# Causal block attention followed by a gated unit: an earlier padding, another first load, joined score groups and a new order

## The chip, the cores and the metric

The kernel runs on one core of a Trainium2 chip. The metric is the device time of one execution in microseconds (us); several executions are timed and their median is given. A profile comes from one further execution, which has a time of its own. The engines are PE (TensorE; its weight loads are a row of their own, PEld), DVE (VectorE), ACT (ScalarE), POOL (GpSimd) and SP (SyncE, which here only issues transfers).

## What is computed

Eight batches, eight heads, 576 tokens, head size 64. Attention is causal by blocks of 64 tokens. Its output, with the heads side by side as 512 features, goes through a unit in which a causal convolution of five taps and a sigmoid gate a linear map, and a second linear map follows. Cut from the reference:

```python
scores = scale * np.matmul(q, k.transpose(0, 1, 3, 2))
mask = block_i >= block_j                      # blocks of 64 tokens
attn = exp(scores - max) / sum                 # where mask
x = (attn @ v) as [8, 576, 512]
gate = sigmoid(sum over kk of conv_w[kk] * x shifted by 4 - kk)
out = (gate * (x @ w_val)) @ w_out
```

## The kernel before

**Units of work.** Four heads form a quad (16 quads, numbered `a`), two heads a pair (32 pairs, `p`). Two batches form a unit of the second half, cut into thirteen token tiles (`n`, 288 tokens wide for n 0 to 3, 384 after that) for convolution, gate and value map, and into 37 output tiles.

**Staging of q and k.** `load_qk` (line 179) brings the 128 x 1152 fp32 block of a quad: partition = (head, group of 18 tokens). `cast_qk` (line 214) turns it into fp16 and, while it does, swaps token and feature so that two neighbouring tokens lie side by side; `trans` (line 242) then transposes these pairs as if they were fp32 elements, 576 of them, in blocks of 32 x 32 on DVE. The result, `qT` and `kT`, has 32 features of a head on each of four strips of 32 partitions. `ends` (line 253) copies the first and the last key block into `kz`, beside zeros. The first quad is loaded, cast and transposed in halves (`load_half`, `cast_half`, `trans_half`, words `Lqh`, `cqh`, `tqh`): each half has 10 or 8 of the 18 tokens of every partition, so all four halves are needed before any score can be made.

**Scores.** `scores` (line 257) computes for quad `a` and key tile `t` (0, 1, 2) the transposed scores of four heads, one on each strip of 32 rows of the PE array, into four PSUM banks. Called with a half index it does the heads of two strips alone. t = 0 takes 448 + 64 + 64 columns a pass, t = 1 takes 448 + 64, t = 2 takes 320 + 192; each twice, as a head has 64 features. `exps` (line 273) turns a bank into 512 fp16 columns of `pt` on ACT. `mask` (line 278) is three POOL instructions a pair: a copy of a 64 x 64 corner into the columns 1536 to 1600, and two clears. `av` (line 289) multiplies with v, a column of ones giving the sums; `norm` divides on DVE; `xtrans` and `evac_x` transpose back into `xts`.

**Second half.** `conv` (line 333) makes the five taps with 32 x 32 diagonal weights, as one unit of 80 matmuls into four banks or as halves of 40 into two; `gate` is a tanh on ACT, `val` the value map, `gated` the product on DVE, `proj`, `evac_out` and `store` the output.

**Order.** Nothing is reordered: the text `PLAN` is a list of words such as `s.4.1.0@56` (scores of quad 4, t = 1, half 0, into banks 5 and 6) and is issued word by word. Each engine takes its own instructions in that order, and SP its transfers. Before the plan come nine matmuls on zeros (`warm`), the identity and its fold (line 434, 437, on DVE) and clears; `pads` (line 418, word `pm`) sets the columns of `pt` behind 1536 to one and the first columns of `xts` to zero, by fourteen POOL instructions inside the plan. All loads are issued by SP.

Of the kernel before, what the change touches and what calls it, by code (L numbers as in the profile page):

```python
# [10 lines left out]
Lqh.0.0 Lqh.1.1  # L11
# [3 lines left out]
Lqh.0.1 cqh.0.0@D tqh.0.0 Lqh.1.0 cqh.1.0@A Lcn cqh.1.1@D cqh.0.1@P w@0 w@0 w@0 w@0 cw@0 tqh.1.1  # L15
Lvt.0 tqh.0.1 tqh.1.0 pm kz.0@P s.0.1.0@12 s.0.2@5634 Lqk.1.1 cvt.0 e.0.1.0 e.0.1.1 e.0.2.3 cT
cq.1.1@P Lqk.1.0 s.0.0.1@70 s.0.1.1@12 Lv.1 e.0.2.2 e.0.1.3 tq.1.1 e.0.0.3 e.0.0.2 kz.1@D cq.1.0@P
s.0.0.0@34 DG cv.1 tq.1.0 e.0.1.2 Lqk.2.1 e.0.0.1 m.1 e.0.0.0 s.1.1.1@07 e.0.2.1 Lqk.2.0 s.1.0.1@12
e.0.2.0 e.1.0.3 e.1.0.2 Lv.0 av.1.0@3 cq.2.1@P av.1.1@4 e.1.1.3 n.1.0 s.1.1.0@56 Lv.3 n.1.1 m.0
e.1.1.2 s.1.2.1@31 cv.0 xtr.1@2 av.0.1@4 e.1.2.3 cq.2.0@P tq.2.1 e.1.2.2 cv.3 av.0.0@0 s.1.0.0@71  # L20
e.1.1.0 Lqk.3.0 Lqk.3.1 Lv.2 m.3 kz.2@D e.1.1.1 e.1.0.1 xt.1 tq.2.0 cq.3.0@P n.0.1 n.0.0 s.1.2.0@23
s.2.2.1@56 Lv.5 e.1.0.0 e.1.2.1 Lvt.1 av.3.0@4 av.3.1@1 Lv.4 s.2.1.1@70 e.1.2.0 s.2.0.1@23 n.3.0
e.2.2.3 cq.3.1@P n.3.1 e.2.2.2 xtr.0@4 tq.3.0 e.2.1.3 cv.2 xtr.3@1 xt.0 tq.3.1 e.2.1.2 s.2.0.0@56
m.2 xt.3 e.2.0.3 s.2.1.0@40 av.2.0@7 cv.5 e.2.0.2 kz.3@D Lqk.4.1 e.2.0.0 n.2.0 e.2.0.1 cvt.1
av.2.1@1 s.2.2.0@23 e.2.1.0 m.5 s.3.2.0@56 n.2.1 cv.4 av.5.0@7 e.2.1.1 e.2.2.0 e.2.2.1 xtr.2@1
av.5.1@0 n.5.0 s.3.1.0@42 Lwv.0 e.3.2.1 cq.4.1@P Lqk.4.0 e.3.2.0 s.3.0.0@37 e.3.1.0 s.3.1.1@56
e.3.1.1 e.3.1.2 n.5.1 xt.2 xtr.5@0 m.4 e.3.1.3 tq.4.1 kz.4@D e.3.0.1 cq.4.0@P e.3.0.0 Lwv.1 xt.5
av.4.1@1 Lv.7 av.4.0@2 n.4.0 n.4.1 s.3.0.1@40 e.3.0.3 s.3.2.1@56 Lqk.5.0 m.6 cn.0.0@23 tq.4.0
e.3.0.2 e.3.2.2 e.3.2.3 wv.1@D cn.1.0@71 th.1.1 th.1.0 wv.0@D s.4.0.0@04 cv.7 s.4.1.0@56 s.4.0.1@17
m.7 th.0.1 th.0.0 e.4.1.0 cq.5.0@P val.0.1@2 av.7.0@3 e.4.1.1 Lqk.5.1 val.1.1@5 e.4.0.2 Lvt.2  # L30
e.4.0.0 val.0.0@6 gv.0.1 n.7.0 cn.0.1@23 e.4.0.1 cq.5.1@P gv.1.1 gv.0.0 tq.5.1 s.4.2@4650 e.4.0.3
th.0.3 th.0.2 s.4.1.1@17 e.4.2.1 Lv.6 e.4.2.0 wv.2@D tq.5.0 val.1.0@2 e.4.1.2 Lqk.7.0 Lvt.3 av.7.1@3
cv.6 Lqk.6.0 av.6.0@4 e.4.1.3 wv.3@P m.8 e.4.2.2 gv.1.0 av.6.1@6 n.7.1 e.4.2.3 Lv.11 s.5.2.1@21
e.5.2.3 Lqk.6.1 n.6.0 cn.1.1@73 kz.5@P e.5.2.2 n.6.1 s.5.1@4056 th.1.2 cvt.3 th.1.3 Lv.8 Lwo.2
e.5.1.1 e.5.1.2 xtr.7@1 xtr.4@2 xtr.6@3 e.5.1.0 cv.11 val.0.2@7 Lv.9 xt.7 val.1.3@1 xt.4 s.5.2.0@20
xt.6 e.5.1.3 Lv.10 e.5.2.1 e.5.2.0 gv.1.3 s.5.0@3456 e.5.0.1 e.5.0.0 cvt.2 gv.0.2 val.1.2@1 gv.1.2
val.0.3@7 cn.3.0@02 cq.6.0@P gv.0.3 tq.6.0 e.5.0.2 cq.6.1@P cv.8 Lwo.1 cn.2@4713 tq.6.1 Lwo.0
e.5.0.3 th.2.3 th.2.2 th.3.1 th.3.0 val.2.2@5 th.2.0 cq.7.0@P th.2.1 av.8.1@6 gv.2.2 m.11 val.2.3@1
m.9 n.8.1 tq.7.0 s.6.1@0235 val.3.0@6 av.11.0@4 cv.9 gv.2.3 Lwo.3 Lqk.7.1 av.9.1@7 cv.10 gv.3.0
e.6.1.3 av.8.0@1 n.11.0 Lqk.8.0 av.11.1@6 kz.6@D e.6.1.1 e.6.1.2 e.6.1.0 wo.1@P wo.0@A s.6.2@4035  # L40
n.9.1 cq.7.1@P e.6.2.3 n.8.0 n.11.1 e.6.2.2 cn.3.1@27 m.10 av.9.0@1 xtr.8@6 e.6.2.0 Lqk.8.1 th.3.2
cq.8.0@P val.3.1@3 e.6.2.1 Lqk.9.1 o.0.0@5 th.3.3 n.9.0 s.6.0@4210 oc.0.0@A xt.8 Lvt.4 gv.3.1 Lv.12
val.2.0@6 Lv.14 tq.7.1 xtr.9@7 val.3.3@3 cq.8.1@P Lv.15 e.6.0.3 gv.2.0 e.6.0.2 xt.9 s.7.1@0156
e.6.0.1 e.6.0.0 av.10.1@7 av.10.0@2 e.7.1.2 tq.8.0 xtr.11@4 m.12 Lv.13 kz.7@P st.0.0 cv.12 gv.3.3
Lqk.9.0 o.0.1@3 e.7.1.3 n.10.1 n.10.0 m.13 e.7.1.1 s.7.0@7256 e.7.1.0 Lqk.10.0 oc.0.1@D xt.11 cv.13
cq.9.1@P cq.9.0@P cv.14 tq.8.1 val.3.2@0 xtr.10@1 Lqk.11.0 av.12.0@3 st.0.1 gv.3.2 Lvt.5 val.2.1@4
e.7.0.2 e.7.0.3 xt.10 s.8.2.1@56 e.7.0.0 e.7.0.1 Lv.17 n.12.0 s.7.2@0127 e.8.2.3 av.12.1@3 gv.2.1
av.13.1@4 n.12.1 kz.8@D Lv.19 e.8.2.2 n.13.1 e.7.2.0 av.13.0@5 o.0.2@6 e.7.2.3 e.7.2.1 n.13.0
cn.4@1430 e.7.2.2 cv.15 oc.0.2@D xtr.12@2 th.4.2 xt.12 th.4.0 cvt.4 xtr.13@7 tq.9.1 th.4.3 th.4.1
m.14 xt.13 o.0.5@5 s.8.2.0@62 oc.0.5@D s.8.0@0314 m.15 Lqk.10.1 Lv.18 o.0.4@7 oc.0.4@D e.8.2.1  # L50
tq.9.0 av.14.1@5 e.8.2.0 o.0.6@2 e.8.0.0 st.0.4 kz.9@P cq.10.0@P e.8.0.1 n.14.1 e.8.0.2 s.8.1@3760
Lv.16 e.8.0.3 cv.17 s.9.1.1@14 oc.0.6@D val.4.2@5 av.14.0@2 e.8.1.3 st.0.2 e.8.1.2 val.4.1@0 gv.4.2
n.14.0 e.9.1.3 cq.11.0@P e.9.1.2 s.9.2@1465 e.8.1.0 e.8.1.1 tq.10.0 m.17 e.9.2.2 st.0.6 av.15.1@2
e.9.2.0 xtr.14@3 e.9.2.3 gv.4.1 av.15.0@7 e.9.2.1 n.15.1 val.4.0@0 cq.10.1@P n.15.0 s.9.1.0@25 m.16
Lqk.11.1 e.9.1.0 cv.19 e.9.1.1 Lqk.12.0 s.9.0@6714 xt.14 gv.4.0 cv.18 Lv.22 av.17.1@3 e.9.0.1
tq.10.1 n.17.1 e.9.0.2 cv.16 e.9.0.3 av.16.0@0 n.16.0 m.19 xtr.15@2 o.0.7@5 o.0.3@3 tq.11.0 e.9.0.0
oc.0.3@A s.10.1@4601 xt.15 Lqk.12.1 e.10.1.3 e.10.1.2 s.10.2.1@72 oc.0.7@D kz.10@P e.10.2.3 e.10.1.1
e.10.1.0 Lv.21 val.4.3@5 e.10.2.2 gv.4.3 cvt.5 cq.11.1@P av.19.0@3 av.16.1@0 o.1.2@1 cq.12.0@P
n.19.0 s.10.0@4653 Lv.20 Lvt.7 n.16.1 oc.1.2@A cv.20 e.10.0.3 e.10.0.2 st.0.7 st.0.5 cn.5@7102
cq.12.1@P th.5.3 m.18 Lv.25 th.5.2 av.17.0@3 tq.11.1 th.5.0 val.5.0@5 th.5.1 e.10.0.0 n.17.0  # L60
val.5.3@0 e.10.0.1 gv.5.3 cn.6@2317 Lqk.14.0 s.10.2.0@04 xtr.17@6 st.0.3 gv.5.0 th.6.3 av.18.1@5
th.6.2 tq.12.0 xtr.16@1 th.6.1 av.19.1@7 th.6.0 e.10.2.1 Lv.23 n.18.1 e.10.2.0 kz.11@D Lqk.13.0
# [38 lines left out]
def kernel(  # L101
# [10 lines left out]
    nc = tc.nc  # L112
# [57 lines left out]
    bank = {}  # L170
# [14 lines left out]
    def half(h):  # L185
        return (slice(0, 5), slice(5, 9))[h]
# [289 lines left out]
```

## Time and profile before

| what | value |
|---|---|
| median of three runs | 189.88 us (189.83, 189.88, 193.27) |
| the profiled execution | 188.78 us, of which 186.9 us from first to last instruction (the span) |
| mean granted TensorE clock in the span | 0.958 |
| busy: PE, DVE, ACT, POOL | 168.9, 131.7, 130.0, 104.3 us |
| first matmul of the scores, first exp | 8.03 us, 8.68 us |
| last matmul ends, last store issued | about 182.7 us, about 183.8 us |

Busy time is the union of an engine's instructions. Matmuls overlap, so what a group of matmuls costs is best read from the start of its first to the start of the next group's first. Times inside the span count from its first instruction.

### The profile page before, as it was taken

The numbers are of one execution on the slowest core, as the hardware profiler recorded it, in microseconds if no ns is written. First come the engines' busy times: TensorE is split into PE (matmuls) and PEld (weight loads), VectorE is DVE, ScalarE is ACT, GpSimd is POOL, SyncE is SP. The second block draws the span as 40 slices with busy tenths as digits, with TensorE's granted clock in tenths as the row PEclk, the third lists the DMA queues.
The fourth block names the chain that finished last, engine by engine and source line by source line (L and its number), as shares of the span: only waits on it lengthen the run. The fifth ranks groups of instructions, "written<-read, shape, count | busy, mean of one in ns | idle before, by whom it ended". The sixth has DMA issues, their size and how long they took to land.

```text
span 186.9 us, 8148 instructions
## 1 busy us (share of the span) xinstructions
PE 168.9 (90%) x3433; PEld 111.0 (59%) x3433; DVE 131.7 (70%) x289; ACT 130.0 (70%) x266; POOL 104.3 (56%) x205
## 2 busy tenths in 40 slices
PE   7635999999996899899999689999999999999991
PEld 2323767776775368456667458666666668654440
DVE  6743997968695579788975588966779677832730
ACT  3393899999998187689898467698779865042342
POOL 4898899599966638788466256929074312000000
PEclk9965799999999699999999999999999999999997
DMA  6999899966999789868987999707861023003685
GB/s 202 287 347 284 226 281 383 365 203 166 238 244 402 186 226 349 208 207 221 346 215 157 262 289 297 206 4 237 257 199 61 22 95 117 4 4 112 239 308 187
DMA packets 49407, 40.39 MB, mean 216 GB/s; under 512 B 39253, under 2 KB 39509, under 8 KB 49370
## 3 DMA queue, kind: packets, MB, share of 16 engines
q1 hardware_dynamic: 49226, 39.73, 70.7%
q8 instruction: 27, 0.44, 1.1%
q10 hardware_dynamic: 144, 0.13, 0.2%
q14 instruction: 10, 0.08, 0.1%
HBM read 30.42 MB, written 9.44 MB: 213 GB/s over the span
## 4 chain that ended last, share of the span: by engine, by line
PE 65%; DVE 16%; DMA 5%; issue 5%; POOL 3%; ACT 2%; SPq 0%; ACTq 0%; DVEq 0%; POOLq 0%
PE B L124 62%; DVE kT L243 4%; PE B L310 4%; DVE qT L243 4%; DMA out_dram<-osb 3%; DVE x L303 3%; DMA qks<-in_q_dram 2%; DVE rc L302 1%; DVE xt L316 1%; DVE gv L359 1%; ACT pt L274 1%; POOL qk L228 1%; POOL pt L420 1%; ACT th L348 1%; DVE osb L228 1%
## 5 line engine op out<-in xcount | busy, mean ns | idle before, releaser
L274 ACT ACTIVATE pt<-B 128x512 f16<-128x512 f32 x192 | 98.3, 620 | 19.1 <-PE B L124 16.6
L228 POOL CAST qk<-qks 128x1152 f16<-128x1152 f32 (+1 forms) x31 | 42.3, 1377 | 5.1 <-DMA qks<-in_q_dram 3.9
L124 PE MATMUL B<-qT,kT 32*128 32x448 f16 (+3 forms) x640 | 39.5, 296 | 5.5 <-DVE qT L243 4.0
L124 PE MATMUL B<-v,pt 128*128 128x65 f16 x896 | 35.9, 195 | 2.9 <-issue 2.5
L124 PE MATMUL B<-xt,w_val 128*128 128x384 f16 (+1 forms) x208 | 37.9, 316 | 0.2 <-issue 0.2
L124 PEld LDWEIGHTS <-pt 128*128 128x128 f16 x960 | 33.8, 99 | 7.0 <-issue 4.7
L124 PE MATMUL B<-w_out,gv 128*128 128x512 f16 (+1 forms) x148 | 35.8, 380 | 2.1 <-DVE osb L228 1.1
L359 DVE SCALAR_TENSOR_TENSOR gv<-th,B 128x384 f16<-128x384 f32 (+1 forms) x52 | 26.1, 518 | 11.8 <-PE B L124 11.3
L303 DVE TENSOR_TENSOR x<-B,rc 128x320 f16<-128x320 f32 x64 | 31.5, 492 | 2.5 <-DVE rc L302 0.2
L124 PEld LDWEIGHTS <-kT 32*128 32x128 f16 x640 | 18.1, 94 | 22.2 <-issue 9.2
L348 ACT ACTIVATE th<-B 128x384 f32<-128x384 f32 (+1 forms) x52 | 20.7, 482 | 13.0 <-PE B L124 7.7
L124 PEld LDWEIGHTS <-w_val 128*128 128x128 f16 x208 | 18.3, 98 | 9.7 <-issue 1.2
L280 POOL COPY pt<-pt 64x128 f16<-64x128 f16 x32 | 10.5, 328 | 22.9 <-ACT pt L274 20.0
L124 PEld LDWEIGHTS <-gv 128*128 128x128 f16 x148 | 13.7, 99 | 15.4 <-issue 3.1
L222 POOL CAST v<-vst 128x512 f16<-128x512 f32 x32 | 19.3, 613 | 5.9 <-DMA vst<-in_v_dram 2.8
L243 DVE STREAM_TRANSPOSE kT<-qk 128x576 f32<-128x576 f32 (+2 forms) x17 | 19.7, 1156 | 4.1 <-POOL qk L228 4.1
L228 ACT COPY osb<-B 128x512 f32<-128x512 f32 (+1 forms) x18 | 10.2, 571 | 16.3 <-PE B L124 15.8
L302 DVE RECIPROCAL rc<-B 128x5 f32<-128x5 f32 x64 | 12.0, 188 | 13.5 <-PE B L124 12.0
L228 DVE COPY osb<-B 128x512 f32<-128x512 f32 x19 | 13.1, 688 | 11.2 <-PE B L124 9.0
L243 DVE STREAM_TRANSPOSE qT<-qk 128x576 f32<-128x576 f32 (+2 forms) x17 | 19.7, 1156 | 0.7 <-PE B L124 0.6
L281 POOL MEMSET pt<- 64x384 f16 x32 | 13.2, 413 | 10.3 <-ACT pt L274 8.8
L316 DVE COPY xt<-B 128x576 f16<-128x576 f16 x32 | 14.1, 450 | 4.5 <-PE B L310 4.5
(42 smaller groups left out, 123.3 us busy)
## 6 DMA issues: line engine op xcount, KB each, us to landing
out_dram<-osb SPq DMA_DIRECT2D x35, 256.0 KB, 2.9
qks<-in_k_dram SPq DMA_DIRECT2D x15, 576.0 KB, 6.7
qks<-in_q_dram SPq DMA_DIRECT2D x15, 576.0 KB, 6.9
vst<-in_v_dram SPq DMA_DIRECT2D x64, 128.0 KB, 5.2
vtst<-in_v_dram SPq DMA_DIRECT2D x8, 128.0 KB, 6.4
w_st<-in_moe_w_val_dram SPq DMA_DIRECT2D x2, 512.0 KB, 6.3
w_st<-in_moe_w_out_dram SPq DMA_DIRECT2D x4, 256.0 KB, 5.1
qks<-in_q_dram SPq DMA_DIRECT2D x1, 320.0 KB, 3.0
```

The source lines that it names most:

```text
L124: nc.tensor.matmul(out=out, lhsT=lhsT, rhs=rhs, start=start, stop=stop, skip_group_check=True)
L222: nc.gpsimd.tensor_copy(out=v16s[p % NV][0:128, 0:4, 0:2, 0:64], in_=vst[p % NVS][0:128])
L228: (eng.copy if eng is nc.scalar else eng.tensor_copy)(out=o, in_=i)
L243: nc.vector.transpose(out=(qT, kT)[i][a % NQT][0:128].bitcast(fp32).rearrange("p c (x n) -> p c n x", n=9)[:, :, n], in_=qk16[(2 * a + i) ...
L274: nc.scalar.activation(out=pts[(2 * a + r // 2) % NPT][0:128, r % 2, 512 * t:512 * t + 512], in_=f32(bank["s", a, t, r]), func=AF.Exp, bia ...
L280: nc.gpsimd.tensor_copy(out=pt[64:128, 0:2, 1536:1600], in_=pt[64:128, 0:2, 0:64])
L281: nc.gpsimd.memset(pt[64:128, 0:2, 0:1536].rearrange("p h (t s) -> p h t s", t=3)[:, :, :, 0:64], 0.0)
L302: nc.vector.reciprocal(out=rc[0:128], in_=O[:, :, 64:65])
L303: nc.vector.tensor_tensor(out=x16[p % NX16][0:128, 0:5, h, 0:64], in0=O[:, :, 0:64], in1=rc[0:128].to_broadcast([128, 5, 64]), op=ALU.mult)
L316: nc.vector.tensor_copy(out=xts[b // 2 % NX][0:128, g, b % 2, 4:4 + SEQ], in_=f16(bank["xtr", p])[:, 0:SEQ])
L348: nc.scalar.activation(out=ths[n % NTH][0:128, r, 0:w], in_=f32(bank["cn", n, r])[:, 0:w], func=AF.Tanh, bias=0.0, scale=0.5)
L359: nc.vector.scalar_tensor_tensor(out=gvs[u % 2][0:128, x, t:t + w], in0=ths[n % NTH][0:128, x, 0:w], scalar=1.0, in1=f32(bank["val", n, x] ...
```

## The change

1. `pads` is gone. The columns 1600 to 1664 of the six `pt` tiles and the first columns of the two `xts` tiles are set by eight DVE instructions before the plan. The rows 0 to 63 of the columns 1536 to 1600 are now filled by `mask`, whose copy takes 128 partitions in place of 64.
2. The first quad is loaded by token ranges: part 0 has the tokens 0 to 255 (8 a partition), part 1 the tokens 256 to 575 (10 a partition). The two parts of q are issued by SP, those of k by ACT, all four before anything else; part 1 comes first on both.
3. A word of `scores` may name two half groups, whose row strips are complementary. Their matmuls are issued in turns, two of one and two of the other. The new plan has 13 such words.
4. Odd quads are cast without the swap and transposed as 1152 fp16 elements; even quads are as before.
5. `PLAN` is new throughout. The four extra warm matmuls are left out; the identity's copies (`id`) stand inside the plan. It has 12 full score words, 46 halves and 13 joined ones (before: 27 full, 42 halves), and 4 full conv words and 18 halves (before: 10 and 6).

```diff
-Lqh.0.0 Lqh.1.1
+Lqh.1.1 Lqh.0.1 Lqh.0.0 Lqh.1.0
...
-Lqh.0.1 cqh.0.0@D tqh.0.0 Lqh.1.0 cqh.1.0@A Lcn cqh.1.1@D cqh.0.1@P w@0 w@0 w@0 w@0 cw@0 tqh.1.1
-Lvt.0 tqh.0.1 tqh.1.0 pm kz.0@P s.0.1.0@12 s.0.2@5634 Lqk.1.1 cvt.0 e.0.1.0 e.0.1.1 e.0.2.3 cT
...
+cqh.1.1@D tqh.1.1 Lcn cqh.0.1@P cw@0 tqh.0.1 cqh.0.0@A tqh.0.0 s.0.2@1234 cqh.1.0@A Lqk.1.0 Lqk.1.1
+tqh.1.0 Lvt.0 kz.0@P Lqk.2.1 cq.1.0@P cq.1.1@P e.0.2.1 Lqk.2.0 cvt.0 cT Lv.1 s.0.1.0@56 e.0.2.0
+e.0.2.3 tq.1.0 tq.1.1 e.0.2.2 Lv.0 cq.2.1@P s.0.1.1@70 s.0.0.1@12 kz.1@D Lqk.3.0 id e.0.0.3 e.0.1.3
+s.0.0.0@34 e.0.1.2 e.0.1.0 e.0.0.2 Lqk.3.1 cq.2.0@P e.0.1.1 Lv.2 e.0.0.0 s.1.2@1207 e.0.0.1 e.1.2.2
+tq.2.1 cv.1 m.1 s.1.0.1@56 s.1.1.0@34 m.0 e.1.2.3 s.1.0.0@07 tq.2.0 cv.0 e.1.2.1 DG e.1.2.0
+s.1.1.1@12 kz.2@D Lv.3 e.1.1.1 e.1.1.0 e.1.1.2 av.1.1@3 cq.3.0@P e.1.1.3 e.1.0.0 av.1.0@4 s.2.2.0@12
...
-    qk16 = ring(NQ16, [128, 9, 64, 2], fp16, "qk16")
+    qk16 = ring(NQ16, [128, 18, 64], fp16, "qk16")
...
+    PARTS = ((0, 8), (256, 10))
+
+    def load_part(i, h, m):
+        t, w = PARTS[h]
+        (nc.scalar if i else nc.sync).dma_start(
+            out=qks[i][0:128, 8 * h:8 * h + w].rearrange("p n d -> p (n d)"),
+            in_=(q, k)[i][0, 0:4, t:t + 32 * w].rearrange("h (x n) d -> h x (n d)", n=w))
...
+    def cast_qk(a, i, m, n=slice(0, 18)):
+        o, s = qk16[(2 * a + i) % NQ16][0:128, n], qks[(2 * a + i) % NQS][0:128, n]
+        if paired(a):
+            o = o.rearrange("p (n e) d -> p n (e d)", e=2).rearrange("p n (d j) -> p n d j", j=2)
+            s = s.rearrange("p (n j) d -> p n d j", j=2)
+        copy(m, o, s)
...
+    def paired(a):
+        return a % 2 == 0
+
+    def trans(a, i, m, h=None):
+        t, w = (0, 18) if h is None else PARTS[h]
+        n = 8 * (h or 0)
+        o, s = (qT, kT)[i][a % NQT][0:128, :, t:t + 32 * w], qk16[(2 * a + i) % NQ16][0:128, n:n + w]
+        if paired(a):
+            o, w = o.bitcast(fp32), w // 2
+            s = s.rearrange("p (n e) d -> p n (e d)", e=2).bitcast(fp32)
+        nc.vector.transpose(out=o.rearrange("p c (x n) -> p c n x", n=w),
+                            in_=s.rearrange("p n (c d) -> p c n d", c=2))
...
+    def scores(*x):
+        *x, m = x
+        if len(x) == 2:
+            parts = [steps(*x, range(4), m)]
+        else:
+            parts = [steps(*x[i:i + 2], (2 * x[i + 2], 2 * x[i + 2] + 1), m[2 * i // 3:2 * i // 3 + 2])
+                     for i in range(0, len(x), 3)]
+        for group in itertools.zip_longest(*parts, fillvalue=()):
+            for w in itertools.chain(*group):
+                mm(*w)
...
-        nc.gpsimd.tensor_copy(out=pt[64:128, 0:2, 1536:1600], in_=pt[64:128, 0:2, 0:64])
+        nc.gpsimd.tensor_copy(out=pt[0:128, 0:2, 1536:1600], in_=pt[0:128, 0:2, 0:64])
...
-    def pads(m):
-        for i in range(NPT):
-            nc.gpsimd.memset(pts[i][0:64, 0:2, 1536:1664], 1.0)
-            nc.gpsimd.memset(pts[i][64:128, 0:2, 1600:1664], 1.0)
-        for i in range(NX):
-            nc.gpsimd.memset(xts[i][0:128, 0:4, 0:2, 0:4], 0.0)
-
-    OPS["pm"] = pads
...
+    for i in range(NPT):
+        nc.vector.memset(pts[i][0:128, 0:2, 1600:1664], 1.0)
+    for i in range(NX):
+        nc.vector.memset(xts[i][0:128, 0:4, 0:2, 0:4], 0.0)
```

(`steps` yields the same matmuls as before, one list for each pass and feature half.)

## Prediction

> **What bounds the kernel now.** I read the 40 slices first, then engine sums by stretch, then the timeline of the first 20 us, then the groups by form and the packets.
>
> ```profile
> PE   7635999999996899899999689999999999999991
> PEclk9965799999999699999999999999999999999997
> ...
> DMA packets 49407, 40.39 MB, mean 216 GB/s; under 512 B 39253, under 2 KB 39509, under 8 KB 49370
> ```
>
> From slice 5 on PE is busy; the holes are at the start (slices 1 to 3), near 60 us and near 105 us. The sums by stretch say whether busy means bound (PE, PEld, DVE, ACT, POOL):
>
> ```profile
> 8.00:16.00 8.00, 3.14 (x58) 1.73 (x60) 3.76 (x4) 6.07 (x12) 7.07 (x16) 0.68 1.03 325
> 16.00:22.00 6.00, 6.00 (x98) 4.50 (x99) 2.91 (x7) 3.26 (x7) 5.01 (x8) 0.57 0.99 291
> 30.00:40.00 10.00, 9.85 (x260) 7.47 (x257) 7.11 (x18) 9.63 (x21) 7.68 (x14) 1.00 1.09 349
> 120.00:130.00 10.00, 10.00 (x206) 6.36 (x204) 6.89 (x15) 8.46 (x18) 6.22 (x13) 1.00 0.33 99
> 150.00:160.00 10.00, 10.00 (x254) 7.43 (x243) 7.61 (x21) 5.77 (x12) 1.64 (x6) 1.00 0.23 84
> ```
>
> From 117 us to the last matmul at 182.7 PE never waits. Up to 60 us ACT and PE are nearly tied. So work added to PE is paid in full in the last third, and a later start is paid too unless PE finds fewer waits.
>
> The start, from the timeline:
>
> ```profile
> 0.72 0.38 SPq L182 DMA_DIRECT2D qks<-in_q_dram  x1
> 8.68 6.07 ACT L274 ACTIVATE pt<-B 128x512 f16<-128x512 f32 x12 [1.53 <-PE B L124]
> 12.07 1.22 DVE L243 STREAM_TRANSPOSE kT<-qk 128x576 f32<-128x576 f32 x1 [4.08 <-POOL qk L228]
> 15.92 1.78 PE L124 MATMUL B<-qT,kT 32*128 32x448 f16 x12 [4.05 <-DVE qT L243]
> 17.95 2.07 ACT L274 ACTIVATE pt<-B 128x512 f16<-128x512 f32 x4 [3.21 <-PE B L124]
> ```
>
> The first quad's twelve exps run at 0.505 us each, then ACT and PE wait for the second quad, which POOL casts late, behind its pads (5.69 to 9.56 us).
>
> **PE's work, counted.** A packed group's price hangs little on how many strips it fills:
>
> ```profile
> 27.40 0.61 PE L124 MATMUL B<-qT,kT 32*128 32x448 f16 x8
> 54.04 0.62 PE L124 MATMUL B<-qT,kT 32*128 32x448 f16 x16
> 50.82 1.75 PE L124 MATMUL B<-xt,DG 32*32 32x288 f16 x120
> ```
>
> Eight matmuls (a half, to the next start at 27.94: 0.54) cost as much as sixteen (next start 54.59: 0.55). Before there are 27 + 42 = 69 such groups, after 12 + 46 + 13 = 71: joining has replaced full groups, not halves. +2 x 0.52 = +1.0. In eight joined words t = 2 meets another t; each step lasts as its wider one, 256 columns more a word (1280 against 1024, 1408 against 1152), by 1024 columns in some 0.45 us 0.11 us: +0.9. Conv: 50.82 to 52.50 holds a half (0.62) and a full unit (1.06); a half ahead of other work costs 0.74. Ten full units become four, so six more are split. One is 288 wide: 2 x 0.68 - 1.06 = +0.3. Five are 384 wide, where a full one costs 1.10 (100.17 to 101.27) and no half was run: between 0.68, as at 288, and 1.10, as a full one; I take 0.88, in proportion to the columns: 5 x (1.76 - 1.10) = +3.3 (bounds +1.3 and +5.5). PE passes between packed and whole-array groups 101 times instead of 93, each entry costing 0.09 (av before av 0.46, before scores 0.56): at most 8 x 0.09, of which half is in the prices above: +0.4. Sum **+5.9 us**, bounds 3.5 and 8.5.
>
> **Pads.** POOL loses some 3.7 us between 5.69 and 9.56; `kz.0` and the casts of quad 1 no longer queue behind them. DVE gains eight short memsets (at most 0.3 each, as POOL's) between 1.1 us and its first cast at 3.7, where it idles once the identity copies (1.7 us) are moved; these come after `kz.1`, ahead of `DG`, which the first conv needs at 35 us. The mask's copy has the same 128 elements a partition (0.33 us): nothing.
>
> **The first loads.** Before, four loads of 320, 256, 256 and 320 KB leave SP at 0.72, 1.17, 1.63 and 2.10 and land 3.0 to 4.2 us later, the last at 6.3. The new ones have the same bytes, but their source runs over 4 heads, then 32 groups. What this does can be read from the packets. The loads and stores of SP and ACT have 36,864 packets of 256 B (64 v loads of 512, 8 of 512); the rest of the 39,253 under 512 B, 2,389, is 149 x 16 + 5. There are 150 transfers: each ends with a tiny packet from every DMA engine that worked on it, 16 of them for all that run over 32, 64 or 128 rows, but 5 for the taps' load, which runs over 5. So a transfer is dealt out by whole outer steps. With 4 outer steps on one side and 128 on the other the row leaves open whether 4 or 16 engines work; I take 4, as equal shares that keep the source's outer steps whole can be no more.
>
> [...]
>
> Price: the best slice moves 402 GB/s, 25 KB/us a DMA engine. Part 1 of q and k, 640 KB, at 100 KB/us takes 6.5 us from the first packet at 1.6: landed at 8.2. Part 0, 512 KB behind them: 13.4. ACT casts both parts 0 ahead of its first exp (640 columns took 0.87, so 512 some 0.72 each): first exp at **14.85** instead of 8.68, and then no break, since quad 1, queued behind on the same four engines (36 KB each a load, 1.5 us: landed 14.9 and 16.4), is ready (POOL's kz at 15.9, its two casts of at most 1.4 to 18.7, DVE's transposes to 20.0) before the twelve exps end at 20.9. In the new order the first `av` stands behind `s.1.1.1`, which needs a bank of the 16th exp: 14.85 + 16 x 0.505 = 22.9, done at 23.4. PE has then done 10 score groups. Before, at 23.4, it had done 11, four `av` (0.46) and one `xtr` (0.28): behind by 0.5 + 1.84 + 0.28 = **2.6 us**. The granted clock, 0.57 from 16 to 22 us, I leave alike, since PE waits early in both. If 16 engines work, the first exp comes at 7.7 (part 1 at 4.6, cast 0.83, DVE's transposes to 6.95, ACT's second cast to 7.7), and PE is ahead by about 2.3 at 16.3 us. Slower DMA engines (before, the first four loads took 4.7 us for 1152 KB, 15 KB/us each) would bring the last part 7 us later still.
>
> **Odd quads.** The fp32 form costs 1.22 us for 576 elements, 0.61 to 0.64 for 256: 1.9 ns each. No 2-byte transpose was run. By bytes 1152 of them cost 1.22, by elements 2.3; I take the first, as the row is nearest in all else. POOL's cast goes from 1.40 for 1152 swapped towards w_out's unswapped 1.04 for 1024, so 1.17: sixteen casts shorter by 0.2, beside PE's work, nothing on the path.
>
> [...]
>
> **New order.** PE's losses after the start are, by starts against usual group times, about 2.0 us in small waits from 22 to 58, 4.2 from 58.7 to 65, 2.3 from 103.8 to 108, and 2.6 elsewhere. Arriving later, PE should meet the first sort ready: -2.0 (bounds 0 and -4.5). The others follow full transfer queues, and the loads are as many: kept.
>
> Sum: +5.9 + 2.6 - 2.0 = **+6.5 us**. Own time of the profiled execution 188.8, so 195.3; the median of the runs is 1.1 above, so **196.4**. The tail stays: ACT still evacuates the last two half tiles.
>
> **Rivals.**
> *All sixteen engines, the same stalls.* For: 128 rows on one side. Then -2.3 + 5.9 - 2.0 = +1.6: 191.5.
> *The early start carries the first third.* ACT's exps begin at 7.7 and never break. Up to the point where PE has 51 us of work, the new order holds 55.7 us of ACT work (93 exps of 0.505, twelve gates, three output copies and two casts), so that point can come at 63.4, against about 71 before; 110.2 of PE work and 4.2 of tail follow: a span of 177.8, plus 0 to 5.5 of later stalls, some 181, 6 less than before: 183.9. It decides once the first exp is before 9 us and ACT idles under 3 us from there to 60. Against it: four outer steps, and the two stalls behind full queues.
> *DVE becomes the bound.* The plain transpose at 2.3 us: sixteen more by 1.1, 17.6 us on DVE's 131.7, of which PE's slack hides about half: some 205.
> *The pads don't matter* is inside the first: then POOL's earlier casts only wait for data.
>
> **How the numbers follow.** Forecast (4 engines) 0.55; all sixteen, same stalls 0.20; early start carries 0.20; DVE bound 0.05. A measurement of this kernel tells about 2% from no change, 3.8 us. Slower by more: 0.50 of the forecast's 0.55, 0.05 of the second, 0.05 of the last: 0.60. Faster by more: 0.18 of the third and 0.02 of the second: 0.20. Within: 0.20. The forecast's own range is 191.5 (PE's work at its low bound 3.5, waits -4.5) to 202 (its high bound 8.5, no wait gone, and part of the slower engines). The whole range, 184 to 202, reaches into the third rival.
>
> **What would show it.** Right: first exp near 14.9, tiny packets of the four first loads 4 each, part 1 landing after 8 us, PE's busy time up by some 5 us, transposes of odd quads near 1.2 us, no PE wait after 120 us. Wrong: the first exp before 9 us (loads on 16 engines), halves of 384-wide conv near 0.68, or PE's stalls near 60 and 105 gone.

## The result and the profile after

| | before | after |
|---|---|---|
| median | 189.86 us (189.61 to 193.27, 4 runs) | 256.49 us (255.18 to 258.54, 4 runs) |
| ratio, 95% interval | | 1.3525 (1.341 to 1.364) |
| profiled execution | 188.78 us, span 186.9 | 255.18 us, span 253.3 |
| DVE busy | 131.7 us | 195.0 us |
| granted TensorE clock, mean | 0.958 | 0.845 |

The kernel is slower, as forecast, but by 66.6 us and not by 6.5: far outside the range of 184 to 202. (The ratios here and below leave out executions that took over 1.5% more than the fastest of their kernel, so a ratio may differ from that of the medians; the profiles of e7, e10 and e13 below are of such executions and are read for the order of events alone.)

The page of the changed kernel: busy sums, slices, and the transfer queue of ACT.

```profile
PE 186.5 (74%) x3429; PEld 121.6 (48%) x3429; DVE 195.0 (77%) x298; ACT 129.6 (51%) x265; POOL 97.3 (38%) x191
...
PE   5026089469908945995699497966999279999994
...
PEclk9555557858975999799779889997999959999999
...
q10 hardware_dynamic: 408, 0.72, 0.9%
```

PE no longer runs through from slice 5: it has holes until the last sixth, and the granted clock is lower with them (mean 0.845, 0.958 before). The sums by stretch (length; busy of PE, PEld, DVE, ACT, POOL; granted clock, transfer share, GB/s):

```profile
8.00:16.00 8.00, 0.00 (x0) 0.00 (x0) 2.32 (x3) 0.00 (x0) 0.85 (x1) 0.50 0.47 128
22.00:32.00 10.00, 1.59 (x24) 0.80 (x20) 9.63 (x2) 4.30 (x9) 6.32 (x10) 0.50 1.07 316
120.00:130.00 10.00, 7.70 (x99) 4.74 (x100) 9.79 (x13) 2.76 (x6) 4.73 (x7) 0.68 0.09 9
224.00:249.00 25.00, 25.00 (x283) 13.10 (x280) 12.64 (x23) 7.99 (x17) 0.00 (x0) 1.00 0.39 144
```

Two rows carry the story. From 22 to 32 us DVE works 9.63 of 10 us on two instructions, and PE does next to nothing. From 120 to 130, where PE never waited before, DVE is at 9.79 and PE waits. Only the end, 224 to 249, is PE's again. The groups of DVE's transposes, by shape (busy us, mean ns):

```profile
L259 DVE STREAM_TRANSPOSE kT<-qk 128x1152 f16<-128x1152 f16 x8 | 41.4, 5179 | 0.4 <-POOL qk L235 0.4
L259 DVE STREAM_TRANSPOSE qT<-qk 128x1152 f16<-128x1152 f16 x8 | 41.1, 5143 | 1.6 <-POOL qk L235 1.6
...
L259 DVE STREAM_TRANSPOSE kT<-qk 128x576 f32<-128x576 f32 x7 | 8.5, 1219 | 0.0
```

A plain transpose takes 5.16 us where the paired one of the even quads takes 1.22: sixteen times 3.94 is 63 us more on DVE. The timeline shows the late start and the first odd quad:

```profile
10.33 0.83 DVE L235 CAST qk<-qks 128x640 f16<-128x640 f32 x1 [8.16 <-DMA qks<-in_k_dram]
...
13.53 0.85 POOL L235 CAST qk<-qks 128x640 f16<-128x640 f32 x1 [10.56 <-DMA qks<-in_q_dram]
...
17.16 1.37 ACT L235 CAST qk<-qks 128x512 f16<-128x512 f32 x2 [13.19 <-DMA qks<-in_q_dram]
...
20.21 2.06 ACT L296 ACTIVATE pt<-B 128x512 f16<-128x512 f32 x4 [1.69 <-PE B L127]
...
22.37 5.11 DVE L259 STREAM_TRANSPOSE qT<-qk 128x1152 f16<-128x1152 f16 x1 [1.58 <-POOL qk L235]
...
27.12 5.29 DVE L259 STREAM_TRANSPOSE kT<-qk 128x1152 f16<-128x1152 f16 x1
...
32.47 1.79 PE L127 MATMUL B<-qT,kT 32*128 32x320 f16 x20 [8.88 <-DVE kT L259]
```

The first exp starts at 20.21 us (8.68 before, 14.85 forecast). Then the two transposes of quad 1 stand one behind the other on DVE, ten microseconds, and PE waits 8.88 us for the second.

### The profile page after: what moved, and what is told of

Same layout as the page of the kernel before. It is cut to its first block, busy times and chain, and to the rows that moved or that the text cites. A ratio compares the mean times of both kernels' runs of the same rounds, so it can differ in the third digit from the quotient of the medians.

```text
span 253.3 us, 8162 instructions
## 1 busy us (share of the span) xinstructions
PE 186.5 (74%) x3429; PEld 121.6 (48%) x3429; DVE 195.0 (77%) x298; ACT 129.6 (51%) x265; POOL 97.3 (38%) x191
## 4 chain that ended last, share of the span: by engine, by line
PE 56%; DVE 19%; issue 13%; DMA 5%; POOL 4%; ACT 2%; POOLq 0%; DVEq 0%; ACTq 0%
PE B L127 52%; DVE qT L259 9%; DVE kT L259 6%; DMA qks<-in_q_dram 5%; PE B L332 4%; POOL qk L235 2%; ACT pt L296 1%; DVE gv L381 1%; DVE xt L338 1%; DVE x L325 1%; POOL v L229 1%; DVE rc L324 1%; POOL pt L302 0%; ACT th L370 0%; POOL kz L235 0%
## 5 line engine op out<-in xcount | busy, mean ns | idle before, releaser
L127 PE MATMUL B<-qT,kT 32*128 32x448 f16 (+3 forms) x640 | 46.8, 334 | 32.8 <-DVE gv L381 15.7
L259 DVE STREAM_TRANSPOSE qT<-qk 128x1152 f16<-128x1152 f16 (+3 forms) x17 | 51.0, 2998 | 6.8 <-POOL qk L235 4.0
L235 POOL CAST qk<-qks 128x1152 f16<-128x1152 f32 (+1 forms) x31 | 38.7, 1259 | 41.4 <-issue 20.6
L259 DVE STREAM_TRANSPOSE kT<-qk 128x1152 f16<-128x1152 f16 (+3 forms) x17 | 51.3, 3020 | 2.0 <-PE B L127 1.6
L127 PE MATMUL B<-v,pt 128*128 128x65 f16 x896 | 39.3, 202 | 13.5 <-DVE xt L338 6.2
L127 PEld LDWEIGHTS <-kT 32*128 32x128 f16 x640 | 20.9, 102 | 53.5 <-issue 26.2
L127 PEld LDWEIGHTS <-pt 128*128 128x128 f16 x960 | 37.1, 103 | 18.5 <-issue 15.3
L127 PE MATMUL B<-w_out,gv 128*128 128x512 f16 (+1 forms) x148 | 38.7, 407 | 0.0
L127 PE MATMUL B<-xt,DG 32*32 32x384 f16 (+1 forms) x1040 | 18.5, 311 | 3.0 <-DVE x L325 3.0
L302 POOL COPY pt<-pt 128x128 f16<-128x128 f16 x32 | 9.4, 294 | 27.3 <-ACT pt L296 27.0
L324 DVE RECIPROCAL rc<-B 128x5 f32<-128x5 f32 x64 | 12.7, 199 | 7.4 <-PE B L127 6.8
```

The costliest lines, as they stand in the source:

```text
L127: nc.tensor.matmul(out=out, lhsT=lhsT, rhs=rhs, start=start, stop=stop, skip_group_check=True)
L235: (eng.copy if eng is nc.scalar else eng.tensor_copy)(out=o, in_=i)
L259: nc.vector.transpose(out=o.rearrange("p c (x n) -> p c n x", n=w), in_=s.rearrange("p n (c d) -> p c n d", c=2))
L324: nc.vector.reciprocal(out=rc[0:128], in_=O[:, :, 64:65])
```

## The experiments

### The odd quads: paired again, and plain alone

Theory A: the plain transposes make nearly all of the loss. Rival B: the loss lies elsewhere. From here on a kernel is named by the first part of its label; e1 is the changed kernel with

```diff
     def paired(a):
-        return a % 2 == 0
+        return True
```

> The changed kernel with every quad in the paired form (cast with the swap, 576 fp32 elements a transpose); all else as changed. Theory A, the plain transposes are the loss: sixteen at 5.16 us become 1.22, DVE's busy time falls from 195 by 63 to some 132 us, the waits for DVE go, and the time falls from 256.5 to 193 to 201 us. Rival B, the order, the joined groups and the first loads are a large part of it: the transposes fall to 1.22 as well, but the time stays above 208 us.

The engine sums on the page of e1:

```profile
PE 174.4 (88%) x3429; PEld 116.4 (59%) x3429; DVE 136.8 (69%) x298; ACT 128.7 (65%) x265; POOL 101.8 (52%) x191
```

Measured: 199.34 us, 1.0415 (1.030 to 1.053) of the kernel before. DVE works 58 us less, and 57.2 us of the 66.6 are gone with one line.

e2 is the kernel before with nothing but the plain form of the odd quads:

```diff
+        if a % 2 == 0:
+            o = o.bitcast(fp32).rearrange("p c (x n) -> p c n x", n=9)[:, :, n]
+            s = s.rearrange("p (n e) d -> p n (e d)", e=2).bitcast(fp32)
+        else:
+            o = o.rearrange("p c (x n) -> p c n x", n=18)
```

> The kernel before with odd quads cast plainly and transposed as 1152 fp16 elements; nothing else changed. Theory A: sixteen transposes at some 5.16 us, DVE's busy time from 131.7 to 191 to 196 us; DVE idled 55 us before, so not all of the 63 us shows: 225 to 250 us. Rival B (a slow transpose is hidden where the order is not the new one): under 208 us.

Measured: 258.98 us, 1.3507 (1.331 to 1.371). Both say A, and e2 more than A had asked: in the old order too the 62 us that DVE has more (16 times 5.11 - 1.22) show in full, 67 us in the time. The expectation had a part of them hidden. None is: a quad's two transposes block for 10 us the queue in which the divisions, evacuations and products stand that give PE its banks back (in e2's trace PE waits 18.6 us for evacuations into `xt` and 11.3 us for products into `gv`), and the mean granted clock falls from 0.958 to 0.833.

### What a 2-byte transpose costs by itself

e3 runs eight forms of the transpose, four of each, with nothing beside them.

> Measures DVE transposes by themselves, four of each form, none of the kernel's computation; the output is one copied tile. Forms: 2-byte 1152 elements with tokens written 18 apart (as in the changed kernel), 4-byte 576 written 9 apart (as before), both with output blocks whole (32 elements in a row), 2-byte 576 written 9 apart, 2-byte 1152 written 2 apart, 4-byte 1152 written 18 apart, 2-byte with the input 18 apart and the output whole. Theory A1, the 2-byte write with a gap between elements is slow: the first is 5.1 to 5.3 us, the 2-byte form with whole output blocks 1.2 to 1.4, the one written 2 apart near 5, the 4-byte forms 1.22 for 576 either way and 2.3 for 1152. Theory A2, any 2-byte transpose of this many elements costs 4.5 ns an element: whole blocks are 5 us too. Theory A3, the distance of 36 bytes is at fault: the form written 2 apart (4 bytes) is fast, 2-byte written 9 apart (18 bytes) differs from 4.5 ns an element.

Measured, us for one: fp16, 1152 elements, writes 36 bytes apart 5.10; the same with whole output blocks 1.38; with writes 4 bytes apart 1.44; half as many elements 18 bytes apart 2.69; whole output, reads 36 bytes apart 2.22; fp32, 576 elements 36 bytes apart 1.20, whole 0.78; 1152 elements 72 bytes apart 2.34. So it isn't the 2-byte element, it is 2-byte writes that lie far apart: theory A3, though its 18-byte form, which it had as another price, costs 4.7 ns an element too. In e12 only that distance changes.

> DVE transposes by themselves, four of each: 1152 elements of 2 bytes whose writes lie 4, 6, 8, 12, 18, 24, 36 and 72 bytes apart (2, 3, 4, 6, 9, 12, 18, 36 blocks of 32 interleaved), then 576 elements of 4 bytes, 8, 12, 24, 36 and 72 bytes apart. The rest of the computation is left out. Theory S, every 2-byte write beyond a short reach is a write by itself: 1.2 to 1.5 us at 4 bytes, 5.1 to 5.3 us from some distance on, with a step between. Rival L, the price grows in proportion to the distance up to 36 bytes and on to 72: some 2.5 us at 18 and 10 us at 72 bytes. For 4 bytes: 0.8 us near, 1.2 us far (by S), or growing (by L).

The timeline of e12, four transposes a line (start, us for four; in the order of the expectation):

```profile
4.99 5.88 DVE L26 STREAM_TRANSPOSE two_a<-s 128x1152 f16<-128x1152 f16 x4
10.78 8.39 DVE L26 STREAM_TRANSPOSE two_b<-s 128x1152 f16<-128x1152 f16 x4
19.02 10.97 DVE L26 STREAM_TRANSPOSE two_c<-s 128x1152 f16<-128x1152 f16 x4
29.80 16.11 DVE L26 STREAM_TRANSPOSE two_d<-s 128x1152 f16<-128x1152 f16 x4
45.63 21.02 DVE L26 STREAM_TRANSPOSE two_e<-s 128x1152 f16<-128x1152 f16 x4
...
107.42 21.13 DVE L26 STREAM_TRANSPOSE two_h<-s 128x1152 f16<-128x1152 f16 x4
128.18 3.39 DVE L26 STREAM_TRANSPOSE four_a<-s 128x576 f32<-128x576 f32 x4
...
144.63 5.11 DVE L26 STREAM_TRANSPOSE four_e<-s 128x576 f32<-128x576 f32 x4
```

Neither S nor L: the price grows along a straight line with the distance, 1.44, 2.08, 2.72, 4.00 us at 4, 6, 8 and 12 bytes, so 0.32 us a byte, and stands still from 18 bytes on (5.1 to 5.2 at 18, 24, 36 and 72). One of the 1152 elements so costs 1.25 ns at 4 bytes and 4.4 to 4.5 from 18 on; the bend lies between 12 and 18 bytes, and no distance between them was run. For 4-byte elements the price is flat from 24 bytes on as well (1.20 at 24 and 36, 1.26 at 72), 2.1 to 2.2 ns for each of 576: so far apart a 2-byte element costs twice a 4-byte one. Why the price stands still there is not shown.

e8 takes the plain form back into the kernel, with a layout in which a partition holds pairs of neighbouring tokens, so that writes lie 4 bytes apart; it also has the loads of e4, below.

```diff
+        for r in range(4):
+            nc.sync.dma_start(
+                out=qks[(2 * a + i) % NQS][32 * r:32 * r + 32].rearrange("p (n j) d -> p n (j d)", j=2),
+                in_=(q, k)[i][a // 2, 4 * (a % 2) + r].rearrange("(n x j) d -> x n (j d)", x=32, j=2))
...
+        for c in range(2):
+            nc.vector.transpose(out=o[:, c].rearrange("p (n x j) -> p n j x", x=32, j=2),
+                                in_=s[:, :, 32 * c:32 * c + 32].rearrange("p (n j) d -> p n j d", j=2))
```

> The kernel with each first load issued by heads; odd quads plain again (no swap in the cast, fp16 transposes), but loaded so that a partition holds the tokens 64 n + 2 x and 64 n + 2 x + 1 (four loads a tensor, rows of 512 bytes), so that the transposes write elements 4 bytes apart in place of 36. Theory A, the distance of the 2-byte writes made the 5.2 us: two transposes of 576 elements a tensor at some 0.72 us each (1.24 ns an element by themselves at that distance, 4.5 at 36 bytes), DVE's work 4 us above that of the kernel with all quads paired, POOL's casts 4 us less, time 189 to 195 us. Rival B, a 2-byte transpose is slow beside the other work whatever its layout: transposes above 2 us each, time above 205 us.

The transposes, by form:

```profile
L270 DVE STREAM_TRANSPOSE kT<-qk 128x576 f16<-128x576 f16 x16 | 12.0, 806 | 1.4 <-POOL qk L242 1.4
```

0.80 us each beside all the other work, two in place of one of 5.16: the distance is the cause, and B's "whatever its layout" falls. The time, 199.05 us (1.0443, 1.037 to 1.051), misses the 189 to 195 all the same. The loads are slower: from 10 to 40 us the transfer share is 1.03 in e8 and in e4, but e8 moves 260 GB/s and e4 316, and POOL's casts wait longer for q (9.3 us in all, 6.4 in e4). Whether the rows of 512 bytes or the four loads a tensor do it isn't told apart. e8's trace also has 5.1 us of the stops in the middle of PE's groups that are described under the new order, e4's 1.8; how the 8 us between the two kernels divide is not shown.

### The first loads, by heads

e4 is e1 with each first load issued as four, one for each head, so that the outer step is 32 groups and not 4 heads:

```diff
-        (nc.scalar if i else nc.sync).dma_start(
-            out=qks[i][0:128, 8 * h:8 * h + w].rearrange("p n d -> p (n d)"),
-            in_=(q, k)[i][0, 0:4, t:t + 32 * w].rearrange("h (x n) d -> h x (n d)", n=w))
+        for r in range(4):
+            (nc.scalar if i else nc.sync).dma_start(
+                out=qks[i][32 * r:32 * r + 32, 8 * h:8 * h + w].rearrange("p n d -> p (n d)"),
+                in_=(q, k)[i][0, r, t:t + 32 * w].rearrange("(x n) d -> x (n d)", n=w))
```

> As the first of these (all quads paired), with each of the four first loads issued as four loads of one head, whose outermost loop has 32 steps. Theory C, the first loads ran on 4 DMA engines since their source has 4 outer steps: now every transfer ends with 16 tiny packets, part 1 lands by 6 us and part 0 by 9 (each load costs some 0.4 us of issue on its queue, 8 a queue), the first exp is near 10 us in place of 20.2, and the time is 4 to 9 us under the run with all quads paired. Rival: 128 rows already went to 16 engines and the second queue is what delayed them: no difference over 1 us.

The page and the timeline of e4:

```profile
q10 hardware_dynamic: 528, 0.72, 1.3%
```

```profile
5.89 0.83 DVE L236 CAST qk<-qks 128x640 f16<-128x640 f32 x1 [3.72 <-DMA qks<-in_k_dram]
...
10.05 1.09 ACT L297 ACTIVATE pt<-B 128x512 f16<-128x512 f32 x2 [1.16 <-PE B L127]
```

Measured: 191.14 us, 1.0047 (0.9975 to 1.0119) of the kernel before. The same bytes over 16 engines bring the first exp from 20.25 (e1) to 10.05 us, and 8.2 us in the time (by the medians; 7.0 by the ratios). The packets settle the count. ACT's queue carries two of the loads and one store: 384 data packets, and 24 tiny ones after (408: 16 of the store, twice 4) against 144 here (528: 16 and eight times 16). The changed kernel, which has the first loads of e1, agrees: from 12 to 16 us, when these loads alone move, the transfer share is 0.26 at 101 GB/s, and four engines of sixteen are 0.25.

With e1 and e4 the loss is accounted for: 57.2 us plain transposes, 8.2 us loads (59 and 7 by the ratios), and nothing that can be told from zero for all the rest.

### Joined scores

e6 writes the thirteen joined words of e4 as two half words each, one behind the other, e.g.

```diff
-s.4.2.0.4.0.1@4263
+s.4.2.0@42 s.4.0.1@63
```

> The kernel with all quads paired and each first load issued by heads, with the thirteen joined score words written as two half words each, one behind the other. Theory P, a packed group costs alike whether it fills two strips or four (as the prediction counted): 26 halves at 0.53 us in place of 13 joined groups at 0.55 to 0.65 make PE's work longer by 5 to 7 us, and as PE bounds the last two thirds, the time is 195 to 198 us. Rival H, two halves of other strips one behind the other overlap on the array and cost what a joined group costs: within 1% of 191.1 us.

Measured: 192.07 us, 1.012 (1.0045 to 1.0195); e4 had 1.0047, the intervals overlap, and P's 195 to 198 is not reached: rival H. In the traces the joined group of this example runs 0.61 us to the next start, the two halves 0.28 + 0.34 = 0.62. So it is in ten of the thirteen places, within 0.02 us: complementary halves overlap on the array when they stand next to each other. In the other three, where a half of t = 0 stands first (`s.8.0.0`, `s.9.0.0`, `s.14.0.0`), the two halves take 0.94 us and the joined group 0.60. By the traces joining is thus worth some 1.2 us in all, less than these times can tell.

### The pads alone

e7 is the kernel before with its pads, at the same place of the plan, on DVE:

```diff
-            nc.gpsimd.memset(pts[i][0:64, 0:2, 1536:1664], 1.0)
-            nc.gpsimd.memset(pts[i][64:128, 0:2, 1600:1664], 1.0)
+            nc.vector.memset(pts[i][0:128, 0:2, 1600:1664], 1.0)
...
-            nc.gpsimd.memset(xts[i][0:128, 0:4, 0:2, 0:4], 0.0)
+            nc.vector.memset(xts[i][0:128, 0:4, 0:2, 0:4], 0.0)
```

with the mask's copy over 128 partitions.

> The kernel before with the pads alone changed: eight memsets by DVE in place of fourteen by POOL, at the same place of the plan, and the mask's copy over 128 partitions. Theory: POOL's two casts of the second quad start up to 3.7 us sooner, the gap of ACT behind the twelfth exp (3.2 us) closes by 2 to 3 us, and as ACT and PE are nearly tied up to 60 us and PE bounds the rest, the time falls by 1 to 3 us against the kernel before. Rival, the casts then wait for their data and the later stalls take the gain back: no change within 0.5%.

Measured: 188.11 us, 0.9876 (0.981 to 0.994) of the kernel before: the lowest ratio here, and clear of 1, but by less than the 2% that the prediction asked for, and from three executions. The mechanism expected is only partly seen. The casts of the second quad start at 10.08 in place of 10.64 us: POOL is free earlier, but then waits 0.60 us for the data, so the start explains 0.6 us of 2.3. In e11, which has the same pads, the second quad's exps start at 17.02 us in place of 17.95. Where the rest comes from stays open. e11 adds to e7 the halves of k on ACT's queue:

```diff
-        nc.sync.dma_start(out=qks[(2 * a + i) % NQS][0:128, n], in_=src[:, n])
+        (nc.scalar if i and n != slice(0, 18) else nc.sync).dma_start(
+            out=qks[(2 * a + i) % NQS][0:128, n], in_=src[:, n])
```

> The kernel before with its pads on DVE, and in addition the two halves of k of the first quad issued by ACT, all four first loads ahead of everything else. Theory: two of the four loads leave 0.9 us sooner, the first exp comes 0.4 to 0.9 us sooner, and this is kept: 0.3 to 1 us below the kernel with the pads alone, 0.982 to 0.986 of the kernel before. Rival: the four loads share sixteen DMA engines and land together as before, 0.988.

Measured: 188.86 us, 0.9898 (0.978 to 1.001); the first exp starts at 9.09, no earlier than before the change. No gain over e7: the rival. With this interval e11 by itself doesn't tell the pads from no change.

### Why the new order doesn't win

e4 loses less to stalls than the kernel before: from 100 to 110 us, where PE worked 7.88 of 10 us before, it works 10.00. Yet it is no faster. Its first third is slow:

```profile
24.00:36.00 12.00, 12.00 (x154) 8.53 (x151) 7.11 (x16) 5.85 (x12) 9.10 (x17) 0.50 1.07 340
40.00:46.00 6.00, 6.00 (x192) 4.77 (x177) 5.12 (x13) 5.27 (x13) 5.25 (x8) 1.00 1.03 282
```

PE is busy without a break from 24 to 36 us, at half rate: 154 matmuls in 12 us, then 192 in 6. In the kernel before `av` is back from 0.82 to 0.45 us, from its start to the next start, at 21 us (the 0.95 of the expectations below is a length, their 0.46 a distance of starts). Theory G: a break of PE brings the half rate, and the half rate eats the gain. Rival D: the transfers set the first third anyway. Five kernels from e4, all with the same words but for these:

```diff
# e5: PE busy ahead of the taps
-cqh.0.1@P cw@0
+cqh.0.1@P w@0 w@0 w@0 w@0 w@0 w@0 w@0 w@0 w@0 w@0 w@0 w@0 cw@0
# e9: the folds and the diagonals behind the first evacuation of x
-e.1.2.1 DG e.1.2.0
+e.1.2.1 e.1.2.0
-xt.1 e.2.2.2
+xt.1 fold DG e.2.2.2
# e10: e9, e5, and seven w@2 ahead of s.1.2@1207
# e13: identity and folds ahead of the plan, diagonals behind the taps
-cvt.0 cT
+cvt.0 cT DG
-Lqk.3.0 id
+Lqk.3.0
# e14: e13, e5, and five w@2 ahead of s.1.2@1207
```

> The kernel with all quads paired and each first load issued by heads, with twelve more matmuls on zeros ahead of the taps, so that PE is busy up to its first scores. In that kernel the granted clock stayed at 0.50 from 9 to 39 us although PE was busy without a break from 24.7 us; in the kernel before it was back at 1.00 at 21 us. Theory G, the clock sets the first third: the clock comes back near 20 us, 16 exps take some 9 us in place of 13 between 30 and 45 us, and the time falls by 3 to 8 us, to 183 to 188 us. Rival D, transfers and ACT set the first third: the clock may come back, the time stays within 1% of 191.1 us. If the clock stays at 0.50 all the same, the run tells only that busy matmuls ahead of the scores don't hold it.

> The kernel with all quads paired and each first load issued by heads, with the four fold copies and the making of the diagonals (DVE, 16.1 to 22.7 us in the traces so far) moved behind the first evacuations of x, some 27 us, still 10 us ahead of the first conv. Theory: PE's gap of 1.2 to 1.9 us near 23 us, in which the first divisions wait behind them on DVE, closes, and the time falls by 0.5 to 1.5 us below that kernel's, to 0.995 to 1.000 of the kernel before. Rival: PE runs at half rate there and something else waits next, no change.

> The same with twelve matmuls on zeros ahead of the taps and seven between the last scores of the first quad and the first of the second, where PE waits 2 us for banks; so PE has work almost without a break from 1 us on. In all kernels with the new order PE's groups took twice their time (av 0.95 in place of 0.46 us) from 15 us until some 37 to 41 us; in the kernel before until 21 us. Theory G, breaks of more than 1 us start and keep the half rate: av takes 0.46 us from the first one at 20 us on, the groups between 24 and 37 us take 6 us less, and the time falls by 3 to 7 us, to 0.96 to 0.985 of the kernel before. Rival D, the groups go at full rate but ACT's exps (0.505 us) and the transfers set the pace up to 40 us: within 1% of the last kernel. Rival N, the half rate comes back in spite of it: then what starts it is not a break of PE.

> The kernel with all quads paired and each first load issued by heads, with the identity's copies and folds ahead of the plan (where DVE idles from 2.2 to 6.0 us) and the diagonals behind the taps (DVE idles from 10.4 to 12.2 us). Theory F, these six DVE instructions, in the new order between the second quad's transposes and the first divisions, make PE's break of 1.2 to 1.9 us near 23 us and with it the half rate that lasts to 37 us: no break after 15.5 us, av back at 0.46 us by 22 to 27 us, and 3 to 6 us less: 0.970 to 0.985 of the kernel before. Rival D, ACT's exps and the transfers set the pace up to 40 us: within 1% of 1.0047.

> The same with twelve matmuls on zeros ahead of the taps and five ahead of the second quad's scores, where PE waits for banks. Theory F: without a break before or after, the groups run at full rate from 16 us on; 0 to 3 us below the last kernel. Rival: the extra matmuls hold up the scores behind them, or the breaks that follow at full rate bring the half rate back: the same or 0 to 2 us above it.

| kernel | ratio to before | granted clock 0.50 in the first 50 us of the trace |
|---|---|---|
| e4 | 1.0047 (0.998 to 1.012) | 8.7 to 39.5 us |
| e5 | 1.0102 (1.005 to 1.016) | 12.7 to 36.6 us |
| e9 | 1.0038 (0.999 to 1.009) | 9.2 to 26.3, 29.7 to 36.5 us |
| e10 | 1.0039 (0.991 to 1.017) | 11.0 to 17.8, 28.1 to 48.5 us |
| e13 | 1.0014 (0.996 to 1.007) | 9.2 to 26.3, 39.9 to 46.7 us |
| e14 | 1.0113 (1.005 to 1.018) | 19.5 to 23.0, 36.6 to 40.0 us |

None of the five reached the time that its theory gave: e5, e9, e10 and e13 are within 1% of e4, and e14 is 1% above e13. In e5 the clock came back at 36.6 us only, so that run tells no more than that busy matmuls ahead of the scores don't hold it; in e10 it came back at 17.8 us and fell again at 28.1 us, behind another break of PE, of 2.36 us.

The break at 22 us did come from the folds and diagonals on DVE ahead of the first divisions: in e9 and e13 it is gone, and the clock is back at 26.3 us. And the half rate did follow longer breaks, though not every shorter one (in e4 PE stops for 1.79 us at 62.1 us and the clock stays at 1.00): in e14 `av` has come back to full rate, then PE stops for 2.47 us and goes on at half rate for 3.5 (start, length; an `av` of 0.96 is one at half rate, of 0.60 at full):

```profile
33.65 0.42 PE L127 MATMUL B<-v,pt 128*128 128x65 f16 x8
36.53 0.47 PE L127 MATMUL B<-v,pt 128*128 128x65 f16 x6 [2.47 <-issue]
36.87 0.96 PE L127 MATMUL B<-v,pt 128*128 128x65 f16 x14
40.28 0.60 PE L127 MATMUL B<-v,pt 128*128 128x65 f16 x14
```

But the time hardly moves. By the start of the same matmul e14 is 7.5 us ahead of e4 where the first conv ends (33.30 and 40.78 us). What is won is lost in this stop, at half rate behind it, and in a later stop of 4.11 us from 57.7 on; soon after that (e4's matmul 995) e14 is 1.4 us behind e4:

```profile
57.24 0.45 PE L127 MATMUL B<-v,pt 128*128 128x65 f16 x9
61.80 0.43 PE L127 MATMUL B<-v,pt 128*128 128x65 f16 x5 [4.11 <-POOL v L230]
```

The transfer share is 1.04 from 30 to 40 us. So G is right that the half rate follows breaks (of 2.36 us in e10, of 2.47 in e14), and wrong in its price. The time is the one that D gave; of its reasons, what these traces show is the two stops, and not ACT's exps.

The stop itself is of a kind that the kernel before has too, at 59 us:

```profile
58.71 0.48 PE L124 MATMUL B<-v,pt 128*128 128x65 f16 x10
61.66 0.28 PE L124 MATMUL B<-v,pt 128*128 128x65 f16 x4 [2.47 <-issue]
```

It comes in the middle of a group, and the trace names no releaser. (At 61.80 in e14 it names POOL's cast of v, but the matmul that ends the stop waits for no semaphore, nine matmuls of that `av` had run before, and the cast had ended at 60.93.) Such stops follow matmul 478 (e8, e9, e13, e14), 733 (e1, e6, e13, e14), 989 (e1, e4, e5, e6, e8, e9, e10, e14), 1118 and 2013 (before) or 2266 (after, e8, e9, e13, e14), among others. Over all traces there are 35 of more than 0.25 us behind the first sixty matmuls, ahead of a matmul that waits for no semaphore, and each lies 90 to 95 above a multiple of 128. e14 has 17 more matmuls than e13 ahead of them, and its stop still follows matmul 478, so that it falls into another `av`: the place went with the count of matmuls, not with the work.

The queue of instructions (q8) moved 27 packets, 0.44 MB, in the kernel before and in e13, so 16 KB each. In every one of the 35 stops PE goes on 1.2 to 1.7 us after a packet of q8 has ended, whether the stop lasts 0.3 or 4.1 us (in the kernel before 1.3 us at 61.66, 1.4 at 105.39). This is an agreement in time: what PE waits for there is not shown, as no run took the packets away. These stops cost 4.1 us in the kernel before, 1.8 in e4 and 7.6 in e14. Why some of them are long is not shown.

## Why the prediction was wrong, step by step

**Odd quads: the step that failed.** "By bytes 1152 of them cost 1.22, by elements 2.3; I take the first, as the row is nearest in all else." It cost 5.16: both ends were too low, and the row was not nearest in what counts. It writes 4 bytes at a time, 36 bytes apart, where the price of 4-byte elements grows little more (e12: 1.20 us at 24 and 36, 1.26 at 72), so it holds the price of a far 4-byte write; nothing in the trace held that of a far 2-byte one. A bound from above was missing, and "nothing on the path" hung on it. With the fp32 row's 2.1 ns for each such write an estimate of the transpose is 2.4 us, still half of what it is. The rival *DVE becomes the bound* named the mechanism, with 0.05 and 205 us; it erred in the same number, and in "PE's slack hides about half" (e2: none). POOL's cast was right: 1.17 forecast, 1.16 measured, as the mean of 30 is 1.273 with fourteen paired ones at 1.40.

**First loads: right mechanism, wrong size.** Four DMA engines, shown by the tiny packets (four a load) and the transfer share of 0.26. The rate was taken at 25 KB/us an engine; the 1152 KB came from 2.2 to 16.9 us, which is 78 KB/us, 20 an engine, so the last part landed 3.5 us later than forecast. Most of the rest is work that the sum left out between ACT's second cast (ended at 18.53) and the first exp: a score group at half rate, 1.7 us. So first exp at 20.21 and not 14.85, and 8.2 us (e4 against e1) where the term had 2.6.

**PE's work.** Halves of 384-wide conv cost 0.66 (e4, median of ten), not 0.88, the low bound's 0.68: 2.2 us less than taken. "Eight matmuls cost as much as sixteen" is true of a half alone and, in ten of thirteen places, not of two complementary ones in a row (e6). Together this step and the order were to give +5.9 - 2.0 = +3.9 us; with the odd quads paired and the first loads on 16 engines (e4), the whole rest gives +0.9 (-0.5 to +2.3). That e1, with the odd quads paired, comes at 199.3 near the forecast of 196.4 is partly luck: its loads cost more than taken, and its matmuls and order less.

**Pads.** Forecast as nothing; alone (e7) they make the kernel before 1.2% faster (0.6 to 1.9%), and e11, with the same pads, is at 1.0% (-0.1 to 2.2%).

**New order.** Stalls behind full queues were "kept": the one near 105 us is gone in e4, the one near 60 is shorter (20 us with 18.21 busy, 17.79 before). "The others follow full transfer queues" missed the stops in the middle of a group: 2.47 us of the one near 60 and 1.04 of the one near 105 lie ahead of a matmul that waits for no semaphore, and end 1.3 and 1.4 us after a packet of q8. "The granted clock ... I leave alike" was wrong: half rate to 39.5 us in e4 in place of 21.

**The end.** "No PE wait after 120 us" fell with DVE's transposes, and holds in e4, where PE works 65.00 of the 65 us from 117 to 182.

## What to carry to other kernels

Price a scattered write by the distance and the size of its elements, not by bytes or elements alone (here 2-byte ones cost 1.25 ns each at 4 bytes and 4.4 to 4.5 from 18 on, 4-byte ones 2.1 to 2.2 from 24 on), and if the trace has no row with that element size at that distance, bound it from above by a run of the instruction alone. An instruction of 5 us on a lightly loaded engine isn't hidden when short work that frees another engine's buffers stands behind it in the queue (e2: 62 us more on DVE, 67 in the time). Give a load an outer dimension of 32, 64 or 128 on both sides, as the loads here that got sixteen engines have, and read from its tiny packets how many it got (here 4 or 16, worth 8.2 us between e1 and e4). Before you explain a stop in the middle of a PE group by data, count the matmuls ahead of it and look at the queue of instructions (35 stops here, each ended 1.2 to 1.7 us after a packet of q8).

## What the runs showed of the hardware

- Writes of DVE's transpose: 1152 elements of 2 bytes cost 1.38 us in whole blocks, 2 bytes apart, 1.44 at 4, then 0.32 us more for each byte up to 4.00 at 12, and 5.1 to 5.2 from 18 to 72; 4-byte elements cost 2.1 to 2.2 ns each from 24 bytes apart on; reads 36 bytes apart 2.22 us against 1.38 for 1152 elements of 2 bytes.
- Half rate outlasts the break by far: in e4 PE was busy without a break from 23.7 to 39.5 us and stayed at half rate all that time, in e9 for 6 us after a break of 1.6, in e14 for 3.5 us after one of 2.5. In the traces' records of the granted clock every stretch but the last is a whole number of 3.41 us long (at half rate nine of them in e4, two in e9, one in e14; in the kernel before 10.24 us from 10.9 on and 3.41 from 62.1 on). What ends the half rate stays open.
- PE stopped in the middle of a group 35 times in fourteen traces, for 0.3 to 4.1 us, each time behind a matmul whose number is 90 to 95 above a multiple of 128, and went on 1.2 to 1.7 us behind a 16 KB packet of q8.
- The row of the granted clock missed the half rate once. e6 has 1.00 in this stretch and as few matmuls as e4 with 0.50:

```profile
24.00:36.00 12.00, 11.99 (x152) 8.60 (x153) 7.39 (x16) 5.99 (x12) 9.30 (x17) 1.00 1.05 336
```

The time of a known group (`av`, start to start, 0.82 or 0.45 us) is the safer clock.
